# A one-token attention block over a 32,768-entry cache: streaming whole heads through three buffers instead of half heads through five

## The chip, the cores and the metric

The kernel runs on one core of a Trainium2 chip. Its engines work side by side, each through its own list of instructions, and wait for one another by semaphores: TensorE (PE in the profile; its weight loads are shown as PEld) multiplies matrices, VectorE (DVE) and ScalarE (ACT) do element-wise work, reductions and 32x32 transposes, GpSimd (POOL) prepares constants, and SyncE (SP) issues the transfers from HBM to the on-chip memory. The metric is the device time of one execution in microseconds (us), the median of several runs. A profile, taken in one further execution, shows what each engine did and when; its "span" runs from the first to the last instruction seen.

## The reference

One token goes through attention over a cache and a small feed-forward block. Only the part that matters for the change is written out:

```python
# x (1,1,512); k_cache, v_cache (1, 8, 32768, 128) bf16; 32 query heads, 4 for each of the 8 cache heads
mod = (silu(c) @ w_mod).reshape(1, 6, 1, -1)        # sa, ca, ga, sb, cb, gb
h = layernorm(x) * (1 + ca) + sa
q = (h @ wq).reshape(1, 1, 32, 128)
scores = einsum('bhqd,bhkd->bhqk', q, k) * 128 ** -0.5   # k repeated 4 times over heads
p = softmax(scores)
o = einsum('bhqk,bhkd->bhqd', p, v)
x = x + ga * (o @ wo)
h = layernorm(x) * (1 + cb) + sb
x = x + gb * (relu(h @ w1) @ w2)
```

Each cache head has 8 MB of K and 8 MB of V. Eight heads are 134 MB, and with the weights 149.4 MB are read once.

## The kernel before

Partition p of the 128 holds keys 256p to 256p+255 of a head, 64 KB of K or V per partition. A head is cut into four key tiles of 64 keys per partition ("u" in the code); two of them are one transfer of 4 MB (32 KB per partition). The transfers go through a ring of five buffers of 32 KB per partition, all on SyncE's queue, in the order of the list `stream` (line 139): the weights `wm` and `wq`, both halves of K of head 0, then alternately half a K of head g+1 and half a V of head g, at the end V of head 7 and the weights `wo`, `w1`, `w2` in small pieces. A buffer is loaded again when what it held has been used. Waits are set by the tile framework.

The stages of a head are:

- `turn_k` (line 405): VectorE transposes K in place in 32x32 blocks, seen as 32-bit pairs, in eight pieces of 128x2048.
- `scores` (line 422): for each piece eight matmuls of 512 columns against `qbd`, a matrix in which the head's four queries stand in a block pattern; a bank of PSUM collects the scores of half a head. `build_qbd` (line 389) fills one of two `qbd` tiles on ScalarE.
- `bank_max` (line 428): VectorE copies the bank to SBUF and takes its maximum.
- `softmax` (lines 437 to 474): maximum over partitions through two small PE transposes, a bias on ScalarE (line 456), the exponential of 1024 columns with its sum (line 459), the transpose of P (line 465), the sum over partitions and its reciprocal. It is written as a generator whose steps are placed among other work.
- `pv` (line 484): 64 matmuls, P as weights (16 columns), V as the moving side (512 columns). For heads 0 to 5 and half of head 6 they are a TensorE loop (line 492) of eight passes with four matmuls each per half head; the rest is written out.
- `blocks`, `o_cols`, `normalise` (lines 513 to 535): pick the diagonal blocks of the result, turn them to columns, divide by the sum.

The order on PE and VectorE is written out by hand (line 599 on): in one round the transposes and scores of head h = g+1 are interleaved piece by piece with the two halves of `pv(g)` and the steps of the softmax. After the last V products follow `project` (output projection; the parts 0 and 1 of `wo` as rows, 2 and 3 as columns), the second layer norm and the feed-forward block. `keep_clock` (line 597) issues matmuls whose result nobody reads.

Of the kernel before, what the change touches and what calls it, by code (L numbers as in the profile page):

```python
# [1 line left out]

# [13 lines left out]

@with_exitstack
def kernel(
    ctx: ExitStack,
    tc: tile.TileContext,  # L20
    A_x: bass.AP,
    A_k_cache: bass.AP,
    A_v_cache: bass.AP,
    A_wq: bass.AP,
    A_wo: bass.AP,
    B_x: bass.AP,
    B_w1: bass.AP,
    B_w2: bass.AP,
    c: bass.AP,
    w_mod: bass.AP,  # L30
    out: bass.AP,
# [10 lines left out]
    NMOD = 6 * KT  # L42
    TK = 64
    NTILE = Sk // (P * TK)
    NG = NTILE // 2

    WOP = [(0, Hkv // 2), (Hkv // 2, Hkv // 4), (Hkv - 2, 1), (Hkv - 1, 1)]
    WOROWS = 2
    LAST = Hkv - 1
    LOOPED = Hkv - 2  # L50
    W2P = [(0, 4), (4, 7), (7, 10), (10, 12), (12, 13), (13, 14)]
    W1P = [(0, KT - 1), (KT - 1, KT)]
    assert Dh == 128 and REP == 4 and D == 512 and FT == W2P[-1][1] and NTILE == 4
    scale = float(Dh) ** -0.5
    eps = 1e-5

# [3 lines left out]
    wm_v = w_mod.rearrange("(p kt) n -> p kt n", p=P)  # L62
    wq_v = A_wq.rearrange("(p kt) n -> p kt n", p=P)
    def wo_v(i):
        g0, n = WOP[i]
        return A_wo[g0 * REP * Dh:(g0 + n) * REP * Dh, :].rearrange("(p r) d -> p r d", p=P)

    w1_v = B_w1.rearrange("(p kt) f -> p kt f", p=P)
    w2_v = B_w2.rearrange("(p f) d -> p f d", p=P)


    front = ctx.enter_context(tc.tile_pool(name="front", bufs=1))
    mask4 = front.tile([P, 32], F32, name="mask4_sb")[:, 0:REP]
    ring = ctx.enter_context(tc.tile_pool(name="ring", bufs=5))
    const = ctx.enter_context(tc.tile_pool(name="const", bufs=1))
    spool = ctx.enter_context(tc.tile_pool(name="spool", bufs=2))
    ps_s = ctx.enter_context(tc.tile_pool(name="ps_s", bufs=3, space=bass.MemoryType.PSUM))
    ps_o = ctx.enter_context(tc.tile_pool(name="ps_o", bufs=2, space=bass.MemoryType.PSUM))
    ps_acc = ctx.enter_context(tc.tile_pool(name="ps_acc", bufs=1, space=bass.MemoryType.PSUM))
    ps_small = ctx.enter_context(tc.tile_pool(name="ps_small", bufs=2, space=bass.MemoryType.PSUM))  # L80

    def small_ps(shape, name):
        return ps_small.tile(shape, F32, tag="small", name=name)


    loaded, last_loop = {}, []

    pieces = {}

    def piece(name, at, n):  # L90

        if name not in pieces:
            pieces[name] = ring.tile([P, 2 * TK * Dh], BF16, tag="slot", name=name)
        return pieces[name][:, at:at + n]

    def load(key):
        kind = key[0]
        if kind == "wm":
            t = ring.tile([P, KT, 6 * D], BF16, tag="slot", name="wm_sb")
            src = wm_v  # L100
        elif kind == "wq":
            t = ring.tile([P, KT, Hq * Dh], BF16, tag="slot", name="wq_sb")
            src = wq_v
        elif kind in "kv":
            g, steps = key[1], key[2]
            src = (kv if kind == "k" else vv)[g, :, TK * steps[0]:TK * (steps[-1] + 1), :]
            name = "Ksb" if kind == "k" else "Vsb"
            if len(steps) == 2:
                t = ring.tile([P, TK * len(steps), Dh], BF16, tag="slot", name=name)
            else:  # L110
                t = piece(name, TK * Dh * (steps[0] % 2), TK * Dh).rearrange("p (j d) -> p j d", d=Dh)
        elif kind == "wo":
            g0, n = WOP[key[1]]
            t = piece("wo_sb", g0 * REP * D, n * REP * D).rearrange("p (r d) -> p r d", d=D)
            src = wo_v(key[1])
        elif kind == "w1":
            k0, k1 = W1P[key[1]]
            t = piece("w12_sb", k0 * Dff, (k1 - k0) * Dff).rearrange("p (kt f) -> p kt f", f=Dff)
            src = w1_v[:, k0:k1]
        else:  # L120
            f0, f1 = W2P[key[1]]
            t = piece("w12_sb", KT * Dff + f0 * D, (f1 - f0) * D).rearrange("p (f d) -> p f d", d=D)
            src = w2_v[:, f0:f1]
        stream_dma(t[:], src)
        if kind in "kv":
            for i, u in enumerate(steps):
                loaded[(kind, g, u)] = t[:, TK * i:TK * (i + 1), :]
        else:
            loaded[key] = t[:]

    def stream_dma(dst, src):
        i = nc.sync.dma_start(out=dst, in_=src)
        tc.stamp_issue_order_token(i.ins, "sp_stream")
        if last_loop:

            tc.add_manual_dep(i.ins, last_loop[0], mybir.DependencyInfo(
                mybir.DependencyClass.NoSync, mybir.DependencyReason.DATA))

    stream = [("wm",), ("wq",)] + [("k", 0, (2 * G, 2 * G + 1)) for G in range(NG)]
    for g in range(LAST):  # L140
        for G in range(NG):
            stream += [(kind, gg, (2 * G, 2 * G + 1)) for kind, gg in (("k", g + 1), ("v", g))]
    stream += [("v", LAST, (0, 1)), ("v", LAST, (2,)), ("v", LAST, (3,))] + [("wo", i) for i in range(len(WOP))]
    stream += [("w1", i) for i in range(len(W1P))] + [("w2", i) for i in range(len(W2P))]
    pos = [0]

    def need(key):
        while key not in loaded:
            load(stream[pos[0]])
            pos[0] += 1  # L150
        return loaded[key]


    wm_sb = need(("wm",))
    cx_row = const.tile([16, D // 8], BF16)
    nc.gpsimd.dma_start(out=cx_row[0:8], in_=c[0].rearrange("(a n) -> a n", a=8))
    nc.gpsimd.dma_start(out=cx_row[8:16], in_=A_x[0, 0].rearrange("(a n) -> a n", a=8))

    ident_bf = const.tile([P, P], BF16)
    make_identity(nc, ident_bf[:])  # L160
    ident_f = const.tile([P, P], F32)
    make_identity(nc, ident_f[:])
    ones_f = const.tile([P, P], F32)
    nc.gpsimd.memset(ones_f[:], 1.0)
    eps_t = const.tile([P, 1], F32)
    nc.gpsimd.memset(eps_t[:], eps)
    sel = const.tile([P, 4, P], BF16)
    ib = ident_bf[:]
    for hp in range(4):
        h, par = hp // 2, hp % 2  # L170
        src = AP(ib.tensor, ib.offset + 64 * h + par, [[ib.ap[0][0], P], [0, 4], [2, 32]])
        nc.vector.tensor_copy(out=sel[:, hp, :].rearrange("p (a c) -> p a c", a=4), in_=src)
    QW = P + 4 * 7
    qbd = [const.tile([P, 4, QW], BF16, name=f"qbd{i}") for i in range(2)]
    nc.gpsimd.memset(qbd[0][:], 0.0)
    nc.gpsimd.memset(qbd[1][:], 0.0)
    onesD_f = const.tile([P, P], F32)
    nc.gpsimd.memset(onesD_f[:], 1.0 / D)
    nc.vector.tensor_reduce(
        out=mask4, in_=ident_f[:].rearrange("p (x q) -> p q x", q=REP), op=ALU.add, axis=AX.X,  # L180
    )

    cmask, rsel = {}, {}
    for n in sorted({n * REP for _, n in WOP}):
        cmask[n] = const.tile([P, P // n], F32, name=f"cmask{n}")
        nc.vector.tensor_reduce(
            out=cmask[n][:], in_=ident_f[:].rearrange("p (c r) -> p c r", r=n), op=ALU.add, axis=AX.X,
        )
        rsel_f = const.tile([P, n], F32, name=f"rsel_f{n}")
        nc.vector.tensor_reduce(  # L190
            out=rsel_f[:], in_=ident_f[:].rearrange("p (c r) -> p r c", r=n), op=ALU.add, axis=AX.X,
        )
        rsel[n] = const.tile([P, n], BF16, name=f"rsel{n}")
        nc.vector.tensor_copy(out=rsel[n][:], in_=rsel_f[:])

    smask = const.tile([16, 4], F32)
    nc.vector.tensor_reduce(
        out=smask[:], in_=ident_f[0:16, 0:16].rearrange("p (s q) -> p s q", q=REP), op=ALU.add, axis=AX.X,
    )
    qsel = mask4[0:16, :]  # L200
    oT_sb = const.tile([P, Hq], BF16)
    oA = [const.tile([P, n * REP, P // (n * REP)], BF16, name=f"oA{i}") for i, (_, n) in enumerate(WOP)]


    place32 = const.tile([P, 32], F32)
    nc.vector.tensor_reduce(
        out=place32[:], in_=ident_f[:].rearrange("p (j m) -> p m j", m=32), op=ALU.add, axis=AX.X,
    )
    rowpick = const.tile([P, KT], F32)
    nc.vector.tensor_reduce(  # L210
        out=rowpick[:], in_=ident_f[:].rearrange("p (j m) -> p j m", m=32), op=ALU.add, axis=AX.X,
    )
    hid_bd = const.tile([P, FT, KT, KT], BF16)
    nc.gpsimd.memset(hid_bd[:], 0.0)
# [25 lines left out]
    def bank(name):  # L240
        return ps_s.tile([P, 512], F32, tag="s", name=name)[:]
# [357 lines left out]
    with tc.manual_schedule(engines={mybir.EngineType.PE, mybir.EngineType.DVE}):  # L599
# [8 lines left out]
        for _ in soft:  # L608
            pass
# [164 lines left out]
```

## Time and profile before

| | us |
|---|---|
| runs | 355.31, 355.36, 355.54; median 355.36 |
| profiled execution | 355.74 |
| its span | 353.94 |
| transposes of K (line 405), 64 | 142.9 busy |
| V products (line 484), 512 | 130.0 busy |
| scores (line 422), 512 | 121.8 busy |
| exponentials (line 459), 8 | 9.2 busy |
| transposes of P (line 465), 8 | 9.7 busy |
| granted PE clock, mean over the span | 0.947 |
| bytes read from HBM | 149.42 MB, 422 GB/s over the span |

In the profile a row such as `152.35 7.11 PE L422 MATMUL ... x32 [0.19 <-PEq L490]` gives the start in the span, the length, the engine, the line, how many instructions were merged, and in brackets how long the engine had been idle and for what it waited. A matmul's own duration (0.38 us for 512 columns) includes its way through the array; the next one starts earlier, so rates are read from starts. "PEclk" or "granted clock" is the share of the full PE clock that was allowed in a stretch. The chain that ended last is followed back from the last instruction, at each step to what released it.

### The profile page before, as it was taken

Reading aid. Unit: us, or ns where it says so; the run is one execution under the profiler, and the core shown is the slowest. Engines: PE = TensorE matmul, PEld = TensorE weight load, DVE = VectorE, ACT = ScalarE, POOL = GpSimd, SP = SyncE. Lnnn points to the kernel's source line nnn. Section 1 sums busy time; section 2 is a strip of 40 time slices with the busy share of each in tenths; the row PEclk is TensorE's granted clock in tenths of the full one; section 3 lists DMA queues with packets and bytes.
Section 4 is the critical chain, followed back from the end, with each engine's and each line's share of the span. In section 5 each row is a group of like instructions: output and inputs, shape, how many; then the busy total and the mean of one; then the engine's idle time right before and its main releaser. Section 6 shows DMA issues by size and latency. Waiting matters only on the chain. (4 is left out here: it accounts for less than half of the span.)

```text
span 353.9 us, 4006 instructions
## 1 busy us (share of the span) xinstructions
PE 279.8 (79%) x1311; PEld 112.7 (32%) x1311; DVE 203.1 (57%) x271; ACT 25.4 (7%) x69; POOL 3.9 (1%) x16
## 2 busy tenths in 40 slices
PE   0542781999898979897979796979689687989996
PEld 0221230333343323332323232323234233334444
DVE  6245775882768268462939178553938095734142
ACT  1220003000010001000100001000100010002000
POOL 4000000000000000000000000000000000000000
PEclk9995997799899999998999899999999997999999
DMA  8999999999999999999999999999999999999994
GB/s 309 455 422 445 431 422 441 441 418 424 459 418 422 459 418 424 441 437 426 433 444 417 430 456 419 427 446 426 422 448 430 422 439 441 422 430 424 421 420 177
DMA packets 6852, 149.59 MB, mean 423 GB/s; under 512 B 824, under 2 KB 1080, under 8 KB 1976
## 3 DMA queue, kind: packets, MB, share of 16 engines
q1 hardware_dynamic: 6776, 149.43, 98.4%
q8 instruction: 8, 0.13, 0.1%
q14 instruction: 4, 0.03, 0.0%
q0 software_dynamic: 64, 0.00, 0.0%
HBM read 149.42 MB, written 0.00 MB: 422 GB/s over the span
## 5 line engine op out<-in xcount | busy, mean ns | idle before, releaser
L405 DVE STREAM_TRANSPOSE Ksb<-Ksb 128x2048 f32<-128x2048 f32 x64 | 142.9, 2281 | 63.9 <-DMA Ksb<-in_A_k_cache_dram 63.9
L484 PE MATMUL o_ps<-Vsb,PT_g 128*16 (+1 forms) x512 | 130.0, 395 | 21.5 <-ACT qbd L389 7.2
L422 PE MATMUL S_ps<-Ksb,qbd 128*128 128x512 bf16 x512 | 121.8, 388 | 23.5 <-DVE Ksb L405 21.9
L422 PEld LDWEIGHTS <-qbd 128*128 128x128 bf16 x512 | 49.0, 98 | 87.6 <-issue 31.8
L484 PEld LDWEIGHTS o_ps<-Vsb,PT_g 128*16 x416 | 37.4, 90 | 90.2 <-issue 63.7
L428 DVE TENSOR_SCALAR_CACHE_REDUCE S_g<-S_ps 128x512 f32<-128x512 f32 x16 | 11.0, 690 | 34.4 <-PE S_ps L422 34.4
L389 ACT COPY qbd<-qrep_sb 32x16 bf16<-32x16 bf16 x32 | 6.4, 201 | 138.7 <-PE S_ps L422 137.6
L465 DVE STREAM_TRANSPOSE PT_g<-P_g 128x1024 bf16<-128x1024 bf16 x8 | 9.7, 1218 | 6.6 <-ACT P_g L459 6.6
L484 PEld LDWEIGHTS <-PT_g 128*16 128x16 bf16 x96 | 8.2, 90 | 11.0
L456 ACT ACTIVATE nbias<-Mb_ps 128x1 f32<-128x1 f32 x8 | 1.4, 171 | 136.8 <-PE Mb_ps L454 136.8
L459 ACT ACTIVATE P_g<-S_g,nbias 128x1024 bf16<-128x1024 f32 x8 | 9.2, 1148 | 0.2
L227 PE MATMUL xc_ps<-cx_sel,cx_bd 16*128 16x2 bf16 x4 | 0.3, 172 | 11.1 <-DVE cx_bd L221 11.1
L515 DVE SCALAR_TENSOR_TENSOR Y<-o_ps,smask,Y 16x128 f32<-16x128 f32 x24 | 8.1, 339 | 0.8
L471 PE MATMUL L_ps<-Lexp,ones_f 128*128 128x4 f32 x16 | 3.0, 257 | 4.3 <-DVE Lexp L468 4.3
L597 PE MATMUL spare_ps<-qbd,ident_bf 128*128 128x512 bf16 x19 | 5.6, 380 | 0.0
L440 PE MATMUL mT_ps<-ident_f,m_p 128*1 128x128 f32 x8 | 2.2, 270 | 3.9 <-DVE m_p L437 2.0
L471 PEld LDWEIGHTS L_ps<-Lexp,ones_f 128*128 128x128 f32 x16 | 3.1, 221 | 5.8 <-issue 5.1
L443 DVE TENSOR_REDUCE Mrow<-mT_ps 1x4 f32<-1x128 f32 x8 | 2.1, 257 | 4.6 <-PE mT_ps L440 4.6
L534 DVE TENSOR_TENSOR oT_sb<-acc_ps,Linv 128x4 bf16<-128x4 f32 x8 | 1.2, 150 | 5.7 <-PE acc_ps L521 5.7
L295 PE MATMUL mod_ps<-wm_sb,siluT 128*1 128x512 bf16 x24 | 3.6, 624 | 1.0 <-DVE siluT L289 1.0
L505 DVE MEMSET o_ps<- 16x512 f32 x8 | 3.9, 485 | 0.8
L552 DVE CAST o_sb<-o_ps 128x4 bf16<-128x4 f32 (+2 forms) x4 | 0.7, 167 | 5.7 <-PE o_ps L548 5.7
(115 smaller groups left out, 80.0 us busy)
## 6 DMA issues: line engine op xcount, KB each, us to landing
Ksb<-in_A_k_cache_dram SPq DMA_DIRECT2D x16, 4096.0 KB, 35.6
Vsb<-in_A_v_cache_dram SPq DMA_DIRECT2D x15, 4096.0 KB, 35.2
wq_sb<-in_A_wq_dram SPq DMA_DIRECT2D x1, 4096.0 KB, 19.6
Vsb<-in_A_v_cache_dram SPq DMA_DIRECT2D x2, 2048.0 KB, 31.8
wm_sb<-in_w_mod_dram SPq DMA_DIRECT2D x1, 3072.0 KB, 10.4
wo_sb<-in_A_wo_dram SPq DMA_DIRECT2D x1, 2048.0 KB, 29.1
w_sb<-in_B_w_dram SPq DMA_DIRECT2D x1, 1344.0 KB
wo_sb<-in_A_wo_dram SPq DMA_DIRECT2D x1, 1024.0 KB, 31.1
```

The costliest lines, as they stand in the source:

```text
L295: nc.tensor.matmul(dst[j // 4][32 * (j % 4):32 * (j % 4) + 1, :], lhsT=src_T[:, kt:kt + 1], rhs=w[:, kt, j * 512:(j + 1) * 512], start=(kt ...
L389: nc.scalar.copy(out=o, in_=i)
L405: t = nc.vector.transpose(out=KTt.bitcast(F32), in_=KTt.bitcast(F32))
L422: nc.tensor.matmul(S_ps_tiles[g], lhsT=qbd[g % 2][:, hp, 4 * (7 - s):4 * (7 - s) + P], rhs=KTv[:, 16 * sl:16 * sl + 16, h, :, par], start= ...
L428: nc.vector.tensor_scalar(out=S_tiles[g][:, G, :], in0=S_ps_tiles[g], scalar1=1.0, scalar2=None, op0=ALU.mult, op1=ALU.max, accum_out=m_ti ...
L459: nc.scalar.activation(out=P_g[:], in_=S_g[:].rearrange("p g f -> p (g f)"), func=ACT.Exp, bias=nbias[:], scale=scale, accum_out=l_g[:],)
L465: nc.vector.transpose(out=PT_g[:], in_=P_g[:])
L471: nc.tensor.matmul(L_ps[:], lhsT=ones_f[:], rhs=Lexp[:], start=True, stop=True)
L484: nc.tensor.matmul(o_tiles[g][:], lhsT=PT, rhs=Vx, start=False, stop=False, skip_group_check=True)
L505: nc.vector.memset(o_tiles[g][:], 0.0)
L515: nc.vector.scalar_tensor_tensor(out=Y[:], in0=o[:, s], scalar=smask[:, s:s + 1], in1=Y[:], op0=ALU.mult, op1=ALU.add,)
L597: nc.tensor.matmul(spare[0], lhsT=ident_bf[:], rhs=qbd[0][:, :, 0:P], start=True, stop=True)
```

## The change

The kernel is rewritten. Everything stands in one critical section: a small class `Flow` records every instruction with what it reads and writes, works out which semaphores each must wait for, and then writes the instructions with explicit waits, engine by engine in the order in which they were recorded. No scheduler moves anything. The arithmetic is the same.

- **Ring.** Three buffers of 64 KB per partition instead of five of 32 KB. A "tenant" is a whole K or V of a head (or the weights). The transfer of tenant i waits for the last uses of tenant i-3. K and V are loaded by one transfer of 8 MB each; V of head 6 comes in two pieces, V of head 7 in three.
- **Order of the stream.** `wm`, `wq`, K0, K1, V0, K2, K3, V1, K4, K5, V2, K6, K7, V3, V4, V5, V6, V7, `wo`, `w1`, `w2`. The first K transfers wait for the two tiny loads of `c` and `x`.
- **Transposes.** Four of 128x4096 per head.
- **Scores.** One TensorE loop per head, which waits for the four transposes of the head and runs eight passes of eight matmuls over both banks; for the last head two loops of half a head. One `qbd` instead of two. The banks are cleared by ScalarE (`clear_s`) and all matmuls add to them.
- **Softmax.** For two heads together: one chain of maxima and PE transposes, two exponentials, which read PSUM directly, one transpose of both P. The copy of the scores to SBUF is gone.
- **V products.** All as TensorE loops: eight passes of eight matmuls (heads 0, 3, 4, 5), sixteen passes of four (heads 1 and 2), and shorter loops for the pieces of heads 6 and 7.
- **Front and end.** The modulation and q are computed by loops with 128-wide weights that hold the vector in one column; the first layer norm stands behind the modulation. Three parts of `wo` are projected as rows instead of two. Temporaries lie in free space of the ring.

The core of the new code (the lines of the old one fall away):

```diff
+ring = const.tile([P, 3 * SLOT], BF16, name="ring")
...
+        def load(self, key, at, n, src, after=()):
+            before = tenants[self.i - 3].uses if self.i >= 3 else []
+            last = {}
+            for o in before:
+                last[o.eng] = o
+            dst = self.ap[:, at:at + n]
+            return op(
+                "sp", lambda: nc.sync.dma_start(out=dst, in_=src), (), [key], after=[*last.values(), *after], dma=True,
+            )
...
+    for g in range(Hkv // 2):
+        order += [("k", 2 * g), ("k", 2 * g + 1), ("v", g)]
+    order += [("v", g) for g in range(Hkv // 2, Hkv)]
+    pieces = {("v", LAST - 1): [(0, 2), (2, 4)], ("v", LAST): [(0, 2), (2, 3), (3, 4)]}
...
+    def turn(h, q):
+        t = K[h]
+        x = t.ap[:, CH * Dh * q:CH * Dh * (q + 1)].bitcast(F32)
+        t.use(dve(lambda: V.transpose(out=x, in_=x), [("k", h, q)], [("kt", h, q)]))
...
+    def scores(h, Gs, ns):
...
+            with T.Fori(0, 9 - ns, ns) as s:
+                for ds in range(ns):
+                    for hp in range(4):
+                        for G in Gs:
...
+                            x = mm(
+                                bank(s_bank(h, G)), qbd[:, hp, 4 * ds:][:, DS(s * 4, P)],
+                                kg[:, ds:][:, DS(s, 1), :, hp // 2, :, hp % 2], False, False,
+                            )
...
+    def maxima(h):
+        i, b = h % 2, s_bank(h, 0)
+        dve(lambda: V.reduce_max(out=m_p[:, i:i + 1], in_=banks[:, b:b + 2, :].rearrange("p g f -> p (g f)"), axis=AX.X),
...
+    def pv(g, us, step):
...
+            with T.Fori(0, 17 - step, step) as jj:
+                for dj in range(step):
+                    for u in us:
...
+    def k_event(h):
+        need("k", h)
+        if summed:
+            sums(summed[0])
+        for u in range(4):
+            turn(h, u)
+            if h == LAST and u % 2:
+                scores(h, (u // 2,), 1 + u // 2)
+        if h < LAST:
+            scores(h, (0, 1), 1)
+        if h + 1 < Hkv:
+            build_qbd(h + 1)
+        if summed:
+            inverse(summed.pop())
+        for g in list(opened):
+            blocks(g)
+            o_cols(g)
...
+        if h % 2:
+            maxima(h - 1)
...
+    def v_event(g, hs, step):
+        need("v", g)
+        open_o(g)
+        maxima(hs[-1])
+        softmax(hs)
+        finish()
+        turn_p(hs)
+        summed.append(hs)
+        clear_s(hs)
+        pv(g, (0, 1, 2, 3), step)
+        opened.append(g)
...
+    for g in range(Hkv // 2):
+        k_event(2 * g)
+        k_event(2 * g + 1)
+        if g + 1 < Hkv // 2:
+            v_event(g, (2 * g, 2 * g + 1), 1 if g else 2)
+    last = (LAST - 1, LAST)
+    need("v", 3)
+    open_o(3)
+    maxima(LAST)
+    pv(3, (0, 1, 2, 3), 2)
+    finish()
+    open_o(4)
+    softmax(last)
+    need("v", 4)
+    pv(4, (0, 1, 2, 3), 2)
+    blocks(3)
+    open_o(5)
+    turn_p(last)
...
+    pv(5, (0, 1, 2, 3), 2)
...
+    pv(6, (0, 1), 4)
...
+    pv(6, (2, 3), 4)
+    blocks(6)
+    pv(7, (0, 1), 4)
...
+    pv(7, (2,), 8)
...
+    pv(7, (3,), 8)
+    blocks(7)
```

More of the change, by code (lines that the diff above doesn't have):

```diff
@@ L17 @@
 @with_exitstack
 def kernel(
[L19 to L31, printed above, removed]
+    ctx, tc, A_x, A_k_cache, A_v_cache, A_wq, A_wo, B_x, B_w1, B_w2, c, w_mod, out,
 ):
@@ L79 @@
[L79 to L129, printed above, removed]
@@ L143 @@
[L143 to L172, printed above, removed]
@@ new lines, in xc_mm @@
+    def xc_mm(inc):
+        for kt in range(KT):
+            i = mm(small[:, 2 * kt:2 * kt + 2], cx_bd.rearrange("a b (m kt) -> a kt (b m)", kt=KT)[:, kt, :], cx_sel)
+        inc(i)
+    first.use(pe(xc_mm, ["tmpB", "cx_sel"], ["b7"]))
+    dve(lambda: V.tensor_copy(
+        out=xc.rearrange("p i kt -> p kt i"), in_=small[:, 0:2 * KT].rearrange("p (kt i) -> p kt i", i=2),
+    ), ["b7"], ["xc"])
+    act(lambda: S.activation(out=e_t, in_=cT, func=ACT.Exp, scale=-1.0), ["xc"], ["e_t"])
+    dve(lambda: V.tensor_scalar(out=e_t, in0=e_t, scalar1=1.0, scalar2=None, op0=ALU.add), ["e_t"], ["e_t"])
@@ L284 @@
-    nc.scalar.activation(out=e_t[:], in_=cT, func=ACT.Exp, scale=-1.0)
-    nc.vector.tensor_scalar(out=e_t[:], in0=e_t[:], scalar1=1.0, scalar2=None, op0=ALU.add)
-    sig = const.tile([P, KT], F32)
-    nc.vector.reciprocal(out=sig[:], in_=e_t[:])
-    siluT = const.tile([P, KT], BF16)
-    nc.vector.tensor_tensor(out=siluT[:], in0=cT, in1=sig[:], op=ALU.mult)
-    def to_rows(dst, src_T, w, n):
-        for kt in range(KT):
-            for j in range(n):
-                nc.tensor.matmul(
-                    dst[j // 4][32 * (j % 4):32 * (j % 4) + 1, :], lhsT=src_T[:, kt:kt + 1],
-                    rhs=w[:, kt, j * 512:(j + 1) * 512], start=(kt == 0), stop=(kt == KT - 1),
-                    skip_group_check=True,
-                )
@@ L368 @@
[L368 to L377 removed]
+        dve(lambda: V.tensor_copy(out=st, in_=sp_), ["b7"], [("st", tag)])
@@ L733, with run @@
+    ffn_ps = bank(3)[0:KT, 0:P]
+    for part, (f0, f1) in enumerate(W2P):
+        def run(inc, part=part, f0=f0, f1=f1):
             for ft in range(f0, f1):
                 for i in range(KT):
-                    nc.tensor.matmul(
-                        ffn_ps, lhsT=hid_bd[:, ft, i, :], rhs=w2_sb[:, ft - f0, i * P:(i + 1) * P],
-                        start=(ft == 0 and i == 0), stop=(ft == FT - 1 and i == KT - 1),
-                    )
-        o_rows = const.tile([KT, P], F32)
-        nc.vector.tensor_tensor(out=o_rows[:], in0=ffn_ps, in1=gb_rows[:], op=ALU.mult)
@@ L741 @@
-        o_bf = const.tile([KT, P], BF16)
-        nc.vector.tensor_tensor(out=o_bf[:], in0=o_rows[:], in1=x1_rows[:], op=ALU.add)
-    nc.sync.dma_start(out=out[0, 0].rearrange("(i n) -> i n", i=KT), in_=o_bf[:])
+                    x = mm(ffn_ps, hid_bd[:, ft, i, :], w2[part][:, ft - f0, i * P:(i + 1) * P],
+                           ft == 0 and i == 0, ft == FT - 1 and i == KT - 1)
+            inc(x)
+        pe(run, [("hid", 0 if f1 <= FT // 2 else 1), ("w2", part)], ["b3"])
+    dve(lambda: V.tensor_tensor(out=o_rows, in0=ffn_ps, in1=gb_rows, op=ALU.mult), ["b3", "gb_rows"], ["o_rows"])
```

996 lines of the change are left out of this document (520 added, 476 removed).

## The prediction

> **What bounds the kernel now.** I read the page first, then the landing times, SyncE's waits, the chain that ended last, and a few stretches of the timeline.
>
> ```profile
> PE 279.8 (79%) x1311; PEld 112.7 (32%) x1311; DVE 203.1 (57%) x271; ACT 25.4 (7%) x69; POOL 3.9 (1%) x16
> DMA  8999999999999999999999999999999999999994
> q1 hardware_dynamic: 6776, 149.43, 98.4%
> ...
> SPq L132 <- PEq L490: 127.1, 13, 11.0
> SPq L132 <- DVE Ksb L405: 103.7, 15, 16.2
> ```
>
> No slice of the DMA row between the first and the last is under 9: the load stream never stands still. SyncE waits long for buffers (127.1 us behind V loops, 103.7 behind transposes), yet each time the next transfer is issued before the running ones are out. The cadence:
>
> ```profile
> 30.48 8.89 DVE L405 STREAM_TRANSPOSE Ksb<-Ksb 128x2048 f32<-128x2048 f32 x4 [5.51 <-DMA Ksb<-in_A_k_cache_dram]
> ...
> 302.99 8.89 DVE L405 STREAM_TRANSPOSE Ksb<-Ksb 128x2048 f32<-128x2048 f32 x4 [4.50 <-DMA Ksb<-in_A_k_cache_dram]
> ```
>
> The first and the last half K tile start their transposes as they land, 28 half tiles apart: (302.99 - 30.48) / 28 = 9.73 us for 4 MB, 19.46 for a head's K or V. So **the stream is the bound**. The end is PE's:
>
> ```profile
> 307.78 7.12 PE S_ps L422 x32
> ...
> 323.70 7.00 PE o_ps L484 x32
> ...
> 347.89 3.30 PE ffn_ps L735 x56
> ```
>
> From 307.78 on PE alone sets the end, but it has only half a head of scores and one and a half of V left, and finishes with the stream. After the last V product (337.8) come 16.1 us to the span's end (353.9). PE has no reserve there: work handed to it later comes out later.
>
> Prices:
>
> ```profile
> 32.80:36.20 3.40, 3.36 (x8) 1.11 (x8) 0.50 1.00 434
> 36.20:41.60 5.40, 5.40 (x25) 2.21 (x23) 1.00 1.09 464
> 62.60:66.90 4.30, 4.30 (x11) 1.48 (x11) 0.50 1.04 450
> ...
> 144.14 8.02 PE L484 MATMUL o_ps<-Vsb,PT_g 128*16 x32 [1.48 <-issue]
> 152.35 7.11 PE L422 MATMUL S_ps<-Ksb,qbd 128*128 128x512 bf16 x32 [0.19 <-PEq L490]
> ...
> 144.13 0.54 PEld L484 LDWEIGHTS o_ps<-Vsb,PT_g 128*16 x4 [1.56 <-issue]
> 145.11 0.58 PEld L484 LDWEIGHTS o_ps<-Vsb,PT_g 128*16 x4 [0.43 <-issue]
> ...
> 163.00:165.90 2.90, 2.90 (x8) 0.93 (x7) 0.50 0.89 384
> ```
>
> The first three rows are windows of line 422 alone, the last one of line 484: stretch, length, PE busy (count), weight loads busy (count), granted clock, DMA share, GB/s. Written out, 32 matmuls take 7.11 us: 0.216 from start to start. In the loop of four a pass takes 0.98 to 1.0 us (loads at 144.13, then 145.11; eight passes in 8.02) against 4 x 0.216 = 0.86. At clock 0.50 a matmul takes 0.427, in the loop too (x8 in 2.90, with parts at the edges): the loop's bookkeeping then vanishes, so it runs ahead of the array when a pass of matmuls outlasts it. After idle stretches the clock is 0.50 for 3.4 and 4.4 us, 8 and 10 matmuls at 0.21 more: 1.7 and 2.1 us a restart.
>
> **The change part by part.**
>
> *Whole heads, whole waits.* K now lands as one 8 MB transfer, and the scores of a head wait for all four of its transposes. Before, PE ran scores half a tile behind DVE. DVE's order per pair of heads is now: transposes K(2g), closing work of the last V, transposes K(2g+1), maxima, then, after the odd head's scores, the second maximum, the joint softmax, the transpose of P, and only then K(2g+2). Behind that second maximum DVE stands still while PE does the odd head's scores. This loop is my forecast:
>
> - transposes: four 128x4096 a head. Upper end twice the pitch of L405, 8 x 2.22 = 17.8; lower end 17.2, if a fixed 0.13 us per instruction (pitch 0.655 for L369's 128x512 against 2.22 for four times that) is paid four times less. I take 17.5.
> - scores: 64 matmuls in passes of eight. Bookkeeping: 0.98 + 4 x 0.15 (spacing of the four loads in 0.54) = 1.6 against 8 x 0.216 = 1.73, so it hides: 14.1 us with entry and drain; with a cold start 1.9 more, 16.0. Upper end, the full loop rate of 8.02 / 32: 16.
> - maximum over 128x1024 from PSUM: two L428 (0.69) less one fixed 0.16: 1.2. From m_p (L437, 53.86) to the end of the bias (L456, 55.28 + 0.17): 1.44 after the maximum. Two Exp (L459 1.15 + 0.18 less overlap): 2.48; transpose of two P: 2 x 1.22 = 2.45; Lexp 0.19. Sum 7.8, the first time 1.28 more for the table load.
> - closing work: four operations on Y and the reciprocal, 1.6.
>
> A round: 17.5 + 1.6 + 17.5 + 16.0 + 7.8 = **60.4 us, against 3 x 19.46 = 58.4 of stream** for K, K, V.
>
> *The clock in time.* Stream start 0.4 later (engines meet once more before the first issue; bounds 0 and 0.7, SyncE's waits at the program's edges), so K0 lands at 30.48 + 9.73 + 0.4 = 40.6, K1 at 60.1. K0 turned 58.1, its scores 74.1; K1 turned 77.6, its scores 93.5; softmax with table load 102.6. Hence DVE starts K2 at 102.6, K4 at 163.0, K6 at 223.4 (landed 99.0, 159.3, 218.4: DVE is late, not the stream). K6 turned 240.9, scores to 256.8.
>
> *The ring of three.* A tile's transfer waits until the tile three before it is wholly used, 2 x 19.46 = 38.9 us after that landed; before there were five half-size buffers and waits by half tiles. From release to landing I add 2.5 to the 19.46 (bounds 1.6: 0.2 to the issue, 0.8 to 1 to the first packet, 0.4 behind the last; and 3.1: wm's 10.4 less 3/4 of 9.73). Behind SyncE's wait stand all later transfers. V(0)'s products end 117.8: V1 could have begun at 118.4, stands 1.9. K6 waits for K4's scores (196.5), V3 for V2's loop (235.8), V4 for K6's scores (256.8): 0.8, 0.4, 1.6. Sum 4.7; V7 lands 337.2, and the 7.5 MB behind it (18.2 us) at 355.4. In the forecast PE is later still, so these stalls cost nothing on top.
>
> *PE's last run.* When K6's scores end (256.8), PE has behind them: K7's scores 16.8 (first half in passes of four, 8 x 0.99 + 0.3, after 1.0 for the rebuilt single qbd; second half 7.6), V3 14.4, V4 15.6 (1.1 for the last softmax's two transposes in front), V5 14.8, V6 and V7 in five loops 31.2. Sum 92.8: the last V product ends at 349.6. Before, K7's scores ended at 314.9 with V6's second half and V7 left; now five V heads are left, because V3 to V7 are put behind all K. The tail takes 16.1 as before, 0.1 for leaving the section: span 365.8, and 1.84 around it (355.74 - 353.9): **367.7**; against the median, 0.4 under the profiled execution, 367.
>
> *At nothing.* Modulation and q as 128-wide matmuls (24 at 0.216 for 0.128, 32 for 0.053: 7 us) with the layer norm behind them (4 us) end near 40 instead of 26.8; the cover is K0's landing (40.6) and K1's (2.0 later than DVE is free); without it, 1 for 1. PSUM banks cleared by ACT (four L307 copies of 0.59, 2.4) lie under 17.5 of transposes. S_g copies (L428) fall away, priced above. Projecting a third part by rows: four matmuls for sixteen of 0.67 in all, within 0.2. Rows of 64 KB instead of 32 save at most 1 us of stream, which is not the bound then. Fewer instructions on PE: PE's sequencer ends no wait of size here.
>
> **Rivals.**
>
> - *Looped matmuls at 0.248 everywhere* (passes of eight no better than of four). For: every warm loop in the trace runs so. Against: the bookkeeping vanishes at half clock. 0.26 more a pass: 1.6 on each of four score loops on the path (K1, K3, K5, K6; two of their eight passes are slow anyway), 2.1 on five V heads, 16.6 in all, less one restart that the shorter idle saves: 382.
> - *Restarts cost next to nothing.* Against it speak the 1.7 and 2.1 us a restart above. For it: behind gaps of 1.8 us V loops of the same form take now 9.04 (at 89.67), now 8.65 us (at 125.65), so not every gap slows the clock. On the path stand four restarts (K1's, K3's, K5's, K6's scores), 7.6 us: 360 without them, 358 with 17.2 per head too. The Trainium skill, "TensorE: Matmul & The Clock Gate", What's actually happening, says the ramp penalty is under 1% of a typical kernel's span and shouldn't be fitted. By that, an estimate, at most 3.6 us over some nine restarts, 1.6 of it on the path: 362. This trace's rows show about half of those 3.6 us in each restart.
> - *Not slower: the wide transposes are cheap.* Place: DVE's two heads a round. The result moves by 6 us per us of a head's transposes. It needs 17.5 - 12 / 6 = 15.5 a head, 0.94 ns an element; then the stream binds again: 355.4 + 0.4 = 355.8, less up to 1 for the longer rows. Against: 1.08 in L405, 1.19 in L465.
>
> **How the numbers follow.** Forecast 0.68 (364 to 373: 17.2 to 17.8 a head, restarts of 1.4 to 2.6), slow loops 0.12, free restarts 0.14, cheap transposes 0.06. Predicted 367. The range 359 to 378 holds the forecast, the free restarts and what lies between the forecast and the slow loops; 0.18 at most is outside. A measurement here can tell about 0.2%, 0.7 us, from no change: the last rival divides into faster 0.03 and same 0.03, slower has 0.94.
>
> **What would show it.** K2's, K4's and K6's transposes starting near 103, 163, 223, each ended idle by the exponential or P's transpose, not by a DMA; DVE idle some 15 us behind the odd head's scores; DMA digits under 9 near 119 and again behind 198; score loops of 14 us warm, with clock 0.50 at their start; PE without a gap from 257 to 350. Wrong if K transposes wait for DMA all along, if looped matmuls run at 0.25, or if PE waits for V at the end.

## The result, and the profile after

The changed kernel takes 366.21 us (median of four runs, 364.59 to 367.27), the kernel before 355.38 us: a ratio of 1.030, 95% interval 1.0255 to 1.0345. It is slower, and 0.8 us under the predicted 367. A second set of six runs gave 366.19 us, ratio 1.0308 (1.0280 to 1.0336).

The profiled execution is the fastest of the first four: 364.59 us with a span of 362.8, so 1.79 around it. The page of it:

```profile
PE 281.1 (77%) x1283; PEld 115.2 (32%) x1283; DVE 195.5 (54%) x187; ACT 31.5 (9%) x69; POOL 4.2 (1%) x17
...
DMA  8998999899988989998999899989998999999970
...
q1 hardware_dynamic: 4760, 149.43, 96.0%
...
PE 49%; DVE 24%; DMA 23%; ACT 2%; issue 1%; POOL 0%; SPq 0%; POOLq 0%
```

PE is busy as long as before (281.1 us for 279.8), DVE a little less, ScalarE 6 us more (31.5 for 25.4, so it is idle most of the time still), and the load queue moves the same 149.43 MB. So the lost time isn't more work on PE, DVE or the queue; the order of waiting is another. The 23% that the last line gives to DMA are the load of `c` and `x`, the transfer of K1 (10.83 to 59.72) and that of K5 (152.92 to 179.33), for whose end DVE waits 0.40 us. The DMA row is a poor witness here: an 8 comes in every fourth slice, also in stretches where the packets of the load queue follow one another without a stop, so the sign that the prediction named (digits under 9 near 119 and behind 198) can't be read from it. The packets themselves show one stop before the end, in front of V1: its last packet ends 22.90 us behind that of the tile before, where the others take 19.32 to 19.36 (19.69 once more, at V5). The last packet ends at 353.1, against 350.2 before.

DVE in the timeline (start, us, what; in brackets the idle time ahead of it and what ended it):

```profile
59.74 17.42 DVE L469 STREAM_TRANSPOSE ring<-ring 128x4096 f32<-128x4096 f32 x4 [1.93 <-DMA ring<-in_A_k_cache_dram]
...
91.66 1.23 DVE L500 TENSOR_REDUCE m_p<-banks 128x1 f32<-128x1024 f32 x1 [12.81 <-PE banks L160]
97.91 2.31 DVE L530 STREAM_TRANSPOSE Pall<-Pall 128x2048 bf16<-128x2048 bf16 x1 [4.13 <-ACT Pall L521]
100.19 17.41 DVE L469 STREAM_TRANSPOSE ring<-ring 128x4096 f32<-128x4096 f32 x4
...
152.88 1.22 DVE L500 TENSOR_REDUCE m_p<-banks 128x1 f32<-128x1024 f32 x1 [14.47 <-PE banks L160]
...
160.13 17.41 DVE L469 STREAM_TRANSPOSE ring<-ring 128x4096 f32<-128x4096 f32 x4
179.36 17.42 DVE L469 STREAM_TRANSPOSE ring<-ring 128x4096 f32<-128x4096 f32 x4 [0.40 <-DMA ring<-in_A_k_cache_dram]
...
218.52 17.41 DVE L469 STREAM_TRANSPOSE ring<-ring 128x4096 f32<-128x4096 f32 x4
```

K0 and K1 wait for their landing. K2, K4 and K6 (100.19, 160.13, 218.52) have no bracket: they follow P's transpose at once, their data is there, and DVE is late. Before that stands the long bracket: 12.81 us (14.47 in the next round) in which DVE has nothing to do but wait for the odd head's scores. The rounds last 59.94 and 58.39 us, where the stream without a stop takes 58.05 for K, K and V. It is not late by much: K2 had landed at 98.42, K4 at 159.98 and K6 at 218.03, so the stream, held up by V1's stop, is only 0.15 us ahead of DVE at K4 and 0.5 at K6.

PE's end in the timeline:

```profile
236.30 15.74 PE L160 MATMUL banks<-ring,qbd 128*128 x64 [4.55 <-DVE Y L573]
...
253.45 16.01 PE L160 MATMUL banks<-ring,qbd 128*128 x64 [1.09 <-ACT qbd L463]
269.38 14.71 PE L160 MATMUL banks<-ring,Pall 128*16 x64
...
299.81 13.98 PE L160 MATMUL banks<-ring,Pall 128*16 x64
...
315.55 0.38 PE L160 MATMUL banks<-mask,Y 16*128 16x4 f32 x2 [1.64 <-DVE Y L576]
316.51 7.07 PE L160 MATMUL banks<-ring,Pall 128*16 x32 [0.58 <-DVE oT_sb L590]
...
345.89 0.38 PE L160 MATMUL banks<-ring,Pall 128*16 x1
```

Scores of K6, scores of K7, then V3 (269.38) to V7: PE works nearly without a stop from 236.30 to the last V product at 345.89. In the kernel before that product started at 337.85:

```profile
337.85 0.38 PE L484 MATMUL o_ps<-Vsb,PT_g 128*16 128x512 bf16 x1
```

No bracket in this stretch names a DMA; what is left of waiting is 1.09 us for the rebuilt `qbd` and DVE's closing work on Y around the first half of V6.

### The profile page after: what moved, and what is told of

Read it like the earlier page. It is cut to its first block, busy times and chain, and to the rows that moved or that the text cites. A ratio compares the mean times of both kernels' runs of the same rounds, so it can differ in the third digit from the quotient of the medians.

```text
span 362.8 us, 4525 instructions
## 1 busy us (share of the span) xinstructions
PE 281.1 (77%) x1283; PEld 115.2 (32%) x1283; DVE 195.5 (54%) x187; ACT 31.5 (9%) x69; POOL 4.2 (1%) x17
## 3 DMA queue, kind: packets, MB, share of 16 engines
q1 hardware_dynamic: 4760, 149.43, 96.0%
## 4 chain that ended last, share of the span: by engine, by line
PE 49%; DVE 24%; DMA 23%; ACT 2%; issue 1%; POOL 0%; SPq 0%; POOLq 0%
PE banks L160 48%; DMA ring<-in_A_k_cache_dram 21%; DVE ring L469 19%; DMA cx_row<-in_A_x_dram 2%; DVE Pall L530 1%; ACT Pall L521 1%; DVE Y L576 1%; DVE m_p L500 1%; ACT L521 0%; DVE Y L573 0%; DVE Mrow L511 0%; ACT qbd L463 0%; PE banks L510 0%; DVE ring L619 0%; PE banks L517 0%
## 5 line engine op out<-in xcount | busy, mean ns | idle before, releaser
L160 PE MATMUL banks<-ring,qbd 128*128 x512 | 122.4, 395 | 40.8 <-DVE ring L469 29.9
L469 DVE STREAM_TRANSPOSE ring<-ring 128x4096 f32<-128x4096 f32 x32 | 139.3, 4410 | 4.3 <-DMA ring<-in_A_k_cache_dram 4.3
L160 PE MATMUL banks<-ring,Pall 128*16 x512 | 120.7, 386 | 10.1 <-DVE Lexp L531 6.5
L160 PEld LDWEIGHTS banks<-ring,qbd 128*128 x512 | 50.6, 99 | 109.8 <-issue 59.8
L160 PEld LDWEIGHTS banks<-ring,Pall 128*16 x512 | 45.2, 89 | 81.7 <-issue 38.1
L500 DVE TENSOR_REDUCE m_p<-banks 128x1 f32<-128x1024 f32 x8 | 9.6, 1203 | 53.1 <-PE banks L160 53.1
L160 PE MATMUL banks<-ring 128*128 x56 | 17.1, 480 | 3.9 <-DVE ring L437 2.4
L530 DVE STREAM_TRANSPOSE Pall<-Pall 128x2048 bf16<-128x2048 bf16 x4 | 9.2, 2312 | 10.0 <-ACT Pall L521 10.0
L521 ACT ACTIVATE Pall<-banks,nbias 128x1024 bf16<-128x1024 f32 x8 | 8.8, 1109 | 0.1
L576 DVE SCALAR_TENSOR_TENSOR Y<-banks,smask,Y 16x128 f32<-16x128 f32 x24 | 8.1, 339 | 0.8
```

What stands on the lines that cost most here:

```text
L160: return T.matmul(o, lhsT=lhsT, rhs=rhs, start=start, stop=stop, skip_group_check=True)
L469: t.use(dve(lambda: V.transpose(out=x, in_=x), [("k", h, q)], [("kt", h, q)]))
L500: dve(lambda: V.reduce_max(out=m_p[:, i:i + 1], in_=banks[:, b:b + 2, :].rearrange("p g f -> p (g f)"), axis=AX.X), [f"b{b}", f"b{b + 1}"] ...
L521: act(lambda h=h, b=b, j=j: S.activation(out=Pall[:, h % 4, :], in_=banks[:, b:b + 2, :].rearrange("p g f -> p (g f)"), func=ACT.Exp, bias ...
L530: dve(lambda: V.transpose(out=pf, in_=pf), keys, keys)
L576: dve(lambda s=s: V.scalar_tensor_tensor(out=Y, in0=o[:, s], scalar=smask[:, 3 - s:4 - s], in1=Y, op0=ALU.mult, op1=ALU.add), [f"b{b}", "Y ...
```

## The experiments

Four questions: is it the serial round of DVE and PE with five V heads behind it (the forecast), the stops of the ring of three, the looped matmuls, or the restarts at half clock? Times are medians, ratios are to the kernel before, which took 355.38 to 355.43 us beside them.

| run | us | ratio, 95% interval |
|---|---|---|
| changed kernel, first and second set | 366.21, 366.19 | 1.0308 (1.0280 to 1.0336), second set |
| x1_half_scores | 361.16 | 1.0145 (1.0118 to 1.0173) |
| x2_v_pass8 | 364.83 | 1.0268 (1.0246 to 1.0289) |
| x3_k_pieces | 360.44 | 1.0132 (1.0107 to 1.0158) |
| x4_no_v3 | 361.59 | 1.0207 (1.0150 to 1.0265) |
| x5_warm | 363.95 | 1.0233 (1.0216 to 1.0250) |
| x6_half_v5 | 356.52 | 1.0030 (1.0018 to 1.0043) |
| x7_no_gap | 364.00 | 1.0245 (1.0228 to 1.0262) |
| x8_all | 357.31 | 1.0060 (1.0043 to 1.0077) |
| x9_v5_only | 366.05 | 1.0301 (1.0286 to 1.0316) |
| x10_turn_early | 401.18 | 1.1286 (1.1269 to 1.1302) |
| x11_turn_early_v5 | 397.97 | 1.1198 (1.1182 to 1.1214) |

**The changed kernel again (x0_after).**

> The changed kernel once more, unchanged, on the same chip as the three below, for a closer baseline: 364.5 to 367.5 by every theory, the spread being restarts at half clock that fall now on K1's scores and now do not (1.7 us each on the path).

366.19 us, six runs from 364.48 to 368.27. In its trace K1's scores took 15.50 us, where they took 14.10 in the first profile, and K2's transposes began at 101.54 for 100.19: the restart fell on the path, as the expectation says. That the whole spread of the six runs (3.8 us) comes from this isn't shown: there is a trace of one run of each set only.

**Scores by halves (x1_half_scores).**

```
-            if h == LAST and u % 2:
-                scores(h, (u // 2,), 1 + u // 2)
-        if h < LAST:
-            scores(h, (0, 1), 1)
+            if u % 2:
+                scores(h, (u // 2,), 2)
```

> Every head's scores as two loops of half a head, each behind its own two transposes; nothing else is moved. Theory (the round of DVE and PE, whole heads waited for, sets the time): PE's half behind the last transposes is 7 to 8.5 us instead of 14 to 16, so a round falls from 59-60 us to the stream's 58.4 or little above, K7's scores end near 262 instead of 269.4, and the time is 358 to 361. Rival (the waits of the ring of three set the end): the transfers wait for the same last uses, the time stays at 365 or more. Second rival (restarts at half clock set it): each head starts two loops behind idle, the gain is under 3 us: 363 or more.

361.16 us, a little above the upper end of the forecast's span and clearly under both rivals. DVE's and PE's timelines of this run:

```profile
99.18 17.42 DVE L469 STREAM_TRANSPOSE ring<-ring 128x4096 f32<-128x4096 f32 x4 [5.81 <-DMA ring<-in_A_k_cache_dram]
...
143.53 1.23 DVE L500 TENSOR_REDUCE m_p<-banks 128x1 f32<-128x1024 f32 x1 [5.87 <-PE banks L160]
```

```profile
293.39 16.29 PE L160 MATMUL banks<-ring,Pall 128*16 x64 [3.59 <-DMA ring<-in_A_v_cache_dram]
```

DVE's wait for the odd head's scores falls from 14.47 (K3) to 5.87, and K2 now waits 5.81 us for its landing: up to here **the round is bound by the stream again**, whose packets have no stop at all (last packet 350.3, as in the kernel before). K7's scores end at 259.8 instead of 269.4. V1's stop is gone with the late round that had caused it: V0's products end at 109.15 instead of 117.50, so the buffer that V1 needs is free in time. So 9.6 us are won there, but only 5 at the end: PE now stands 3.59 us before V5, for a DMA, and begins it at half clock (16.29 for 13.98). (The 5 us are between the medians; these two traces differ by 2.8, since this one is of the slowest of its four runs and the first profile of the fastest.)

**V1 and V2 in passes of eight (x2_v_pass8).** Edit: `v_event(..., 1 if g else 2)` becomes `v_event(..., 2)`.

> The V products of heads 1 and 2 in passes of eight matmuls instead of four. Theory (the round sets the time): their loops fall from 17.7-18.0 to about 14.2 us, but they end long before the next scores can start, so the time changes by less than 1 us. Rival (loops of four are what the change costs): 3.5 to 7 us less, 358 to 362.

The two products fall from 17.98 us, with the small matmul behind them, to 15.8; K4 starts at 159.88 for 160.13, K6 at 218.61 for 218.52, and the span is 362.7 for 362.8. The median is 1.4 us lower, more than the 1 us expected, but the intervals overlap and the spans agree, so no gain is shown. The loops of four cost 2.1 us each where nothing waits for it.

**K as two transfers (x3_k_pieces).**

```
-        for a, b in pieces.get((kind, g), [(0, 4)]):
+        for a, b in pieces.get((kind, g), [(0, 2), (2, 4)] if kind == "k" else [(0, 4)]):
```

> Each head of K is loaded as two transfers of half a head; scores still wait for a whole head. K tiles have landed before DVE is free for them in most rounds, so by the theory only K0 and K1 gain: K0's transposes start at about 31 instead of 40.4 but wait for the qbd and the prologue only with their scores; K1's still wait for its landing (second half 59.7, two transposes of 4.4 behind it), so K1's scores end some 8 us earlier, 83 instead of 91.6, and the whole chain behind moves up by 7 to 9 us until it meets the stream: 357 to 360. Rival (stalls of the ring set the end): 365 or more, since the transfers and their last uses stay in order.

360.44 us, just outside. DVE began K0 at 38.39, not 31: until then the prologue stands ahead of it in DVE's list. K0's and K1's transposes then follow each other without a stop (34.72 us for both), K2 starts at 96.13, 4.1 us earlier. K2, K4 and K6 in DVE's timeline of this run:

```profile
96.13 17.41 DVE L469 STREAM_TRANSPOSE ring<-ring 128x4096 f32<-128x4096 f32 x4
...
155.70 17.41 DVE L469 STREAM_TRANSPOSE ring<-ring 128x4096 f32<-128x4096 f32 x4
...
215.11 17.41 DVE L469 STREAM_TRANSPOSE ring<-ring 128x4096 f32<-128x4096 f32 x4
```

The rounds are as long as before, 59.57 and 59.41, and DVE doesn't wait for K once: the lead of 4 us passes through them (K6 3.4 us earlier, as is the end of this trace; the medians differ by 5.8). This says the same as x1 from the other side: a round of some 59.5 us is made by DVE and PE alone.

**V3 left out but for a pass (x4_no_v3).** Edit: `pv(3, (0, 1, 2, 3), 2)` ends after the first of its eight passes.

> The V product of head 3 does one of its eight passes and leaves out the other seven eighths of its matmuls. Theory (from K7's scores on PE alone sets the end): 12.5 us less on PE, the end falls until the last V tile's landing binds (stream end 353.0 in the run above, 349.3 before): 355 to 358. Rival (the stream, or the tail, sets the end already): less than 2 us.

361.59 us: neither. PE in the timeline of this run:

```profile
277.01 15.81 PE L160 MATMUL banks<-ring,Pall 128*16 x64 [4.51 <-DMA ring<-in_A_v_cache_dram]
...
296.21 4.05 PE L160 MATMUL banks<-ring,Pall 128*16 x18 [2.76 <-DMA ring<-in_A_v_cache_dram]
```

PE has 12.8 us less to do and gives most of it back before V4 and V5, which land whole at 276.7 and 295.9 here. The last V product starts at 342.3 instead of 345.9. So there is a **second limit 3.6 us under the first**: the landing of V5 as one tile, and everything that PE has to do behind it. The expectation had overlooked it. V1's stop is part of this landing: in x1, without the stop, V5 lands at 293.0. (The expectation's 349.3 for the stream's end before is too low as well: the last packet ends at 350.2.)

**PE kept busy before the scores (x5_warm).**

```
+    def warm(h):
+        def run(inc):
+            for _ in range(18):
+                x = mm(bank(6)[:, 128:512], ident_bf, qbd[:, 0:3, 0:P])
+            inc(x)
+        pe(run, ["ident_bf", "qbd", ("kt", h, 2)], ["junk"])
...
             turn(h, u)
+            if u == 2 and h < LAST:
+                warm(h)
```

> 18 matmuls of 384 columns into a part of bank 6 that nothing reads are put behind the third transpose of every head but the last, so that PE is busy (2.9 us at full clock, some 4.6 after a stop) until the fourth transpose ends. Theory: K3's scores (15.76 us) and K6's (16.05) begin at full clock and take 14.1; both lie on the path, and K5's and K1's were at full clock already, so PE's last run starts 3.6 us earlier. It then meets the landing of V5 (PE waits for it in the run without head 3's V product, where the last V product started at 342.3 instead of 345.9), so 361.5 to 364. Rival (a restart costs next to nothing): 365 or more.

363.95 us, in the span, at its upper end: 2.2 us under the changed kernel, and the interval doesn't meet that of the second set. K3's and K6's scores take 14.1 us now. (K6's had taken 15.74; the 16.05 in the expectation is K0's.) K4 gains nothing by it: its transposes then wait 1.48 us for the landing, which V1's stop has delayed (they start at 160.81). So by the medians restarts do cost on the path, 2.2 us of 366.2 in this kernel. Where the gain arises isn't shown: this trace is of the slowest of its four runs, V6's first loop ran at half clock in it (8.76 us for 7.07), and its last V product starts no earlier than in the first profile (346.35 for 345.89).

**V5 by halves, scores by halves (x6_half_v5).**

```
-    pieces = {("v", LAST - 1): [(0, 2), (2, 4)], ...
+    pieces = {("v", 5): [(0, 2), (2, 4)], ("v", LAST - 1): [(0, 2), (2, 4)], ...
...
-    pv(5, (0, 1, 2, 3), 2)
+    pv(5, (0, 1), 4)
+    pv(5, (2, 3), 4)
```

> Scores by halves as in x1_half_scores, and V of head 5 as two transfers and two loops. Theory: with the scores by halves PE's end was set by V5's landing as a whole (idle 289.8 to 293.4, then a loop of 16.3 instead of 14.0 us behind the stop): with V5 by halves PE goes on at once, the last V product starts 4 to 6 us earlier, the stream (its end was 350.3, as in the kernel before) and PE end together: 355 to 357.5. Rival (what is left is the serial tail and DVE's steps between the V loops): less than 2 us under x1_half_scores.

356.52 us, 4.6 under x1 and 9.7 under the changed kernel. PE's timeline:

```profile
289.60 13.98 PE L160 MATMUL banks<-ring,Pall 128*16 x64
...
347.79 1.74 PE L160 MATMUL banks<-ring,hid_bd 128*4 128x128 bf16 x28 [0.16 <-DMA ring<-in_B_w_dram]
```

PE goes from V4 to V5 (289.60) without a wait, and at the end the last layer waits for its weights: the stream is the bound, with its last packet at 350.4 for 350.2 before. What is left of the difference is 0.2 us there and 0.5 between that packet and the end of the span (4.2 for 3.7); before's own profiled execution was another 0.4 over its median. This version still has the ring of three buffers and K as whole transfers of 8 MB, so neither costs much by itself: what cost were the wait of a head's scores for the whole head and V5 as one tile.

**V5 by halves alone (x9_v5_only).** The edit of x6 without that of x1.

> V of head 5 as two transfers and two loops, scores by whole heads as in the changed kernel. Theory (two limits one behind the other): PE comes to V5 at 299.8, when it has landed for 4.5 us, so nothing is waited for and the time changes by less than 1 us. Rival (whole V transfers cost by themselves, with or without the round of scores): 3 to 5 us less, as between the two runs with scores by halves (361.2 and 356.5).

366.05 us: no change. With scores by whole heads PE comes to V5 too late to wait for it. The two edits together bring 9.7 us, one alone 5, the other alone 0: two limits, one behind the other.

**DVE's steps ahead of PE's (x7_no_gap).**

```
     pv(5, (0, 1, 2, 3), 2)
-    spread(0)
-    blocks(4)
+    blocks(4)
+    spread(0)
...
     normalise(5)
-    spread(1)
     pv(6, (2, 3), 4)
+    spread(1)
```

> The four operations on Y of head 4 are put ahead of the copy behind the first spread, and the second spread behind the second half of V6; no operation is added or left out. Theory: PE's waits for DVE inside its last run (313.9 to 315.55, 315.9 to 316.5, 323.9 to 324.4: 2.8 us) vanish, and since nothing else is late there the time falls by 2.3 to 2.8 us: 362 to 364. Rival (the landing of V6 or V7 is as late as PE): less than 1 us.

364.00 us, 2.2 less. From V5's first product to the last V product PE takes 43.9 us in this trace for 46.1 in the first profile: PE alone sets the end there, and its small waits pass straight to it.

**All of it (x8_all).** The edits of x1, x2, x3, x6 and x7, and one `Exp` behind the first norm.

> Together: scores by halves, K and V5 as two transfers, V1 and V2 in passes of eight, the order of x7_no_gap, and one Exp behind the square root of the first norm so that the table is there before the first softmax. Theory: the stream is the bound again, as in the kernel before, with its start 0.2 to 0.4 us later: 354.5 to 356.5, within 0.3% of the kernel before. Rival (something of the change that none of these undoes, a tail longer by over 1 us): 357 or more.

357.31 us, the rival's side, and 0.8 over x6. In its trace PE is so early that it waits 4.24 us for V4 and starts it at half clock (16.40), and the last packet ends at 351.3, 0.9 later than in x6. The span ends 4.2 us behind that packet, as in x6, so it isn't the longer tail of the rival: the stream itself is later. The delay is there in full when K7 has landed (235.87 for 234.99): the halves of K come mostly 9.71 us apart, 19.42 a head, where whole heads take 19.35, and K in two transfers is the only edit that touches the stream up to there. More haste ahead of a stream that is the bound bought nothing. None of these versions is faster than the kernel before.

**DVE's idle time filled (x10_turn_early, x11_turn_early_v5).**

```
-            turn(h, u)
+            if u > 1 or h % 2 or h == 0:
+                turn(h, u)
...
         open_o(g)
+        need("k", 2 * g + 2)
+        turn(2 * g + 2, 0)
+        turn(2 * g + 2, 1)
         maxima(hs[-1])
```

> Scores by whole heads; the first two transposes of K2, K4 and K6 are put ahead of the second maximum, into the time in which DVE stands idle behind the odd head's scores. Theory (the round is serial because DVE idles there): 8.8 us of transposes move under the scores, a round falls from 59-60 us to the stream's 58.4, K7's scores end about 262 to 264 and V5's landing sets PE's end: 360 to 362, as with scores by halves. Rival (the ring of three buffers or the whole-head wait itself is the cost): 365 or more.

> The early transposes of the run before, V5 as two transfers and two loops, and the order of x7_no_gap. Theory: both limits are gone and the stream is the bound: 355.5 to 357.5. Rival (scores by halves are needed, since PE still has a whole head of scores behind K7's or K6's transposes): 358 or more.

401.18 and 397.97 us: both far off, and the cause lies in the edit itself. DVE in the timeline of x10:

```profile
99.32 8.77 DVE L469 STREAM_TRANSPOSE ring<-ring 128x4096 f32<-128x4096 f32 x2 [20.31 <-DMA ring<-in_A_k_cache_dram]
108.02 1.18 DVE L500 TENSOR_REDUCE m_p<-banks 128x1 f32<-128x1024 f32 x1
...
174.68 8.77 DVE L469 STREAM_TRANSPOSE ring<-ring 128x4096 f32<-128x4096 f32 x2 [20.39 <-DMA ring<-in_A_k_cache_dram]
```

The idle time can't be filled with K2, because K2 lands only at 99: V0 is loaded between K1 and K2. The transposes that were put ahead hold DVE's queue for 20.3 us, and behind them stand the maximum, the softmax, V0's products and with these the buffer that V1 is waiting for. The stream now really stops (V1 lands 36.70 us behind K3, V2 and V3 31.4 and 31.3 us behind the tile before them), so the rounds grow to 75.4 and 70.2 us. So these two runs don't test what they were made for, but they show what the ring of three costs when a release is late: 35.0 us for three rounds in x10.

## Why the prediction was right, point by point

**The bound moved as forecast.** K2, K4 and K6 without a wait for DMA, DVE idle behind the odd head's scores, PE alone at the end: all are in the first profile, and x1, x3 and x9 show that these, not the stream, made the time. With V1's stop the stream is nearly as late, though (K4 landed 0.15 us ahead of its turn, where the forecast had 3.7), and x5 ran into it.

**The terms.**

| term | predicted | measured (profiled execution) |
|---|---|---|
| four transposes of a head | 17.5 | 17.42 |
| scores, from a stop / at full clock | 16.0 / 14.1 | 15.7 to 16.05 / 14.10 |
| maximum over 1024 | 1.2 | 1.20 |
| K3's scores to K4's first transpose (maximum to P) | 7.8 | 7.3 |
| a round | 60.4 | 59.94, 58.39 |
| K2, K4, K6 start | 102.6, 163.0, 223.4 | 100.2, 160.1, 218.5 |
| K6's scores end to the last V product | 92.8 | 93.9 |
| from there to the end of the span | 16.2 | 16.9 |
| span | 365.8 | 362.8 |

The scores of K1, K3 and K5 in PE's timeline of the first profile:

```profile
77.53 14.10 PE L160 MATMUL banks<-ring,qbd 128*128 x64 [3.31 <-DVE ring L469]
...
137.08 15.76 PE L160 MATMUL banks<-ring,qbd 128*128 x64 [3.52 <-DVE ring L469]
...
197.14 14.10 PE L160 MATMUL banks<-ring,qbd 128*128 x64 [3.01 <-DVE ring L469]
```

The start of K6 is 4.9 us early for three reasons: K1's and K5's scores found the clock at full speed (1.4 and 1.5 us less from the last transpose to the end of the scores than the 16.0 forecast), the chain through the softmax is 0.5 shorter each of the three times, and small terms (K1 landed 0.4 earlier, a head's transposes take 0.1 less) make the rest, less 0.4 for K5's wait for its landing. K1's was chance: in the second set's trace K1's scores took 15.50 and K2 started at 101.5. PE's last run gave back 1.1, mainly in two places: K7's scores took 0.6 longer with their slower passes of four, and V6 and V7 0.9 longer, since PE has three waits for DVE there, 2.7 us in all, that the prediction didn't list (x7 got 2.2 of them back). The end gave back 0.7.

**The number was partly luck.** The sum forecast 367.7 us for the profiled execution, which took 364.59, 3.1 less. The 0.4 taken off for the median had the wrong sign here, as the median of 366.21 lies 1.6 above that execution. The mechanism came out as forecast, but the 0.8 us between the predicted 367 and the median is less than these misses, and less than the spread of 3.8 us between runs of the kernel.

**Mis-sized terms.** "Passes of four" were put at 0.99 us; they take 1.08 to 1.11 (V1: 17.66 us for 16 passes at full clock), for which nothing waits but in K7's first half. V1's stop was put at 1.9 us and is 3.5; its place was right, the buffer came free at 117.5 (forecast 117.8) and V1's first packet starts at 118.49. But from release to landing it took 23.1 us, 3.75 over a tile's 19.35, where 2.5 (at most 3.1) had been added, and the tile before had landed 0.6 earlier than forecast. The three other stops (0.8, 0.4, 1.6) don't come in this execution: its rounds are shorter than forecast, so buffers come free earlier. "At nothing on top" held to 0.4 us, K5's wait. The longer rows brought 0.02 us a head against the kernel before (19.34 for 2 x 9.68), and 0.07 against the halves of K in x8; both stay under the 1 us allowed for the whole stream. One reading was off: the pitch of L369 is 0.64 us in the trace, not 0.655, which puts the lower end of a head's transposes at 17.3 instead of 17.2 and changes nothing else.

**The rivals.** Slow loops fall: a loop in passes of eight takes 14.10 us for 64 matmuls, 0.218 from start to start, as written out. Cheap transposes fall: 17.42. Free restarts fall as a price of nothing: K3's scores take 15.76 where K5's take 14.10. With all four on the path at full clock, as in x5's trace, the median is still 363.95, not the 360 that this rival gave: K4's landing stands behind them. The Trainium skill's bound in "TensorE: Matmul & The Clock Gate", What's actually happening, under 1% of a kernel's span for the ramp, agrees with the whole that x5 won by keeping PE busy (2.2 us, 0.6%); it doesn't agree with leaving the restarts out of this sum, where the two on K1 and K5 decided 2.9 us of 366.

**What the prediction didn't see** is the second limit. It followed PE's last run, which did set the end, and not what would bind when that run is shortened: V5 lands as one tile, and from its first product to the last V product PE has 46.1 us to do (299.81 to 345.89), with the tail behind that.

## What to carry to other kernels

A wait for a whole tile costs the work that could have run under the rest of the tile: look at which engine stands idle behind the last piece, and count that time into the round; here scores by whole heads made a round 59.9 and 58.4 us long, where the stream needs 58.05, made the release of a ring buffer late, and left PE 94 us of work behind K6's scores. When a limit is removed, look for the next one before expecting its whole size: the two edits that mattered gave 5.0 and 0 us alone and 9.7 together. An idle engine isn't free time for work whose data lands later: put into an in-order queue, such work turned some 13 us of idle time a round into a loss of 35 over three rounds.

## What was not expected of the hardware

Whether a stop slows TensorE's clock isn't told by its length. The stretch from 78 to 80 us, K1's first matmuls, in the first profile of the changed kernel and in x7_no_gap (stretch, length, PE busy (count), weight loads, DVE, ACT, POOL, granted clock, DMA share, GB/s):

```profile
78.00:80.00 2.00, 2.00 (x11) 0.91 (x10) 0.76 (x2) 0.00 (x0) 0.00 (x0) 1.00 0.46 197
```

```profile
78.00:80.00 2.00, 2.00 (x7) 0.63 (x6) 0.86 (x2) 0.00 (x0) 0.00 (x0) 0.50 0.71 262
```

The stop ahead of them was 3.31 us in the first, which ran on at 1.00, and 2.37 us in the second, which fell to 0.50. In four traces K1's stop was 3.16 to 3.33 us without a slower clock, in four others 2.37 to 2.74 with one, and in x3 it was 1.94 without. The place of the stop decides: in each of the fourteen traces, all changes of the granted clock lie on a grid of 3.41 us, and where the grid lies differs from one execution to the next. In the four traces with a slower clock, 2.22 to 2.42 us of K1's stop lie in one step of the grid, and the clock falls at the end of that step; in the five without, the grid divides the stop so that no step holds more than 1.82 us of it. For other stops the border is not as sharp (the clock fell at the end of steps with only some 1.5 us idle, and stayed through one with 2.03), so this is no full rule. The Trainium skill, "TensorE: Matmul & The Clock Gate", What's actually happening, names a window that runs by itself and isn't started by the kernel; that the same code falls now on one side and now on the other agrees with it, but its idle time of about 3.4 us for a fall doesn't agree with the 2.37.
